# A gated mix of long convolution and local attention: the second half of the attention heads on blocks of 57 queries by 64 keys, in a new hand-written order

## The chip, the cores and the metric

The kernel runs on one core of a Trainium2 chip. Five engines work side by side and meet through semaphores: PE (TensorE, the matrix multiplier, whose weight loads are shown apart as PEld), DVE (VectorE), ACT (ScalarE), POOL (GpSimd) and SP (SyncE, which here only issues DMAs). PE writes only to PSUM, and ACT and DVE carry its results from there into SBUF. The metric is the device time of one execution in microseconds (us).

## The reference

Two branches share the input `x = A_q` (2048 rows, 640 columns) and are mixed row by row by a gate. Branch A multiplies a shifted key by a value, convolves the product over the whole sequence (an FFT in the reference) and multiplies by `q`. Branch B is attention with 32 heads of 20 columns, in which every query sees only 8 keys: its own row and the rows 2, 4, ... 14 above it.

```python
x = A_q
g = sigmoid((x * gate_w).sum(-1, keepdims=True))
# A: k_shift = 4-tap causal convolution of A_k; kv = k_shift * A_v
#    y = causal convolution of kv with ssm_k over 2048 rows (rfft, product, irfft, cut to S); y = y + kv * ssm_D
a = x * y
# B: q, k, v = x @ wqkv in 32 heads of 20
logits = einsum("bhsd,bhswd->bhsw", q, kg) * 20 ** -0.5     # kg: keys at s, s-2, ... s-14
o = einsum("bhsw,bhswd->bhsd", softmax(masked logits), vg)
b = o.reshape(B, S, D) @ wo
return g * a + (1 - g) * b
```

## The kernel before, in words

The even rows and the odd rows of `x` form two sequences of 1024, so that a query's keys are 8 neighbours. Attention cuts each sequence into 9 blocks of 114 queries (`BQ`), and a block needs 121 keys (`BK`): its own 114 and the 7 ahead of them. There are 18 blocks (`NB`) and 8 *sets* `t` of four heads. A set's keys and queries lie in `kb` and `qb`, the four heads at partitions 0, 32, 64 and 96, 20 rows of data and 11 rows of a mask each (`mm`): the mask makes the score of every pair outside the band so negative that its exponential is zero.

For a set, `score_gen` (L637) multiplies keys by queries into PSUM, 121 keys on the partitions by 114 queries on the columns, the four heads as four tiles of 32 rows of the array (L647); the 18 blocks go in five groups of 4, 4, 4, 3 and 3. ACT takes the exponential of each group in two instructions, two heads in each (L658), 912 or 684 columns of 121 partitions, into one of 9 slots (`NET`) of `ETall`. `pv_gen` (L664) uses each piece of `ETall` as the weights of a matmul whose moving operand is the head's 20 value columns and a column of ones (`VW`, L682; the extra columns of the next heads that it takes along are overwritten). DVE takes the reciprocal of the ones' column (L692) and multiplies (L694) into `oS`, which lies over `VW`. Matmuls at L652 write to columns that nobody reads.

The values `VW` are made by `vproj` (L526), one half of the heads each (`hp`), the keys and queries by `qkproj` (L573) into `stg`, from where DMAs on POOL's queue (on SP's for the first) place them into `kb` and `qb` (`fragger`, L623). When all sets are done, `op_tr` (L861) transposes `oS` through PE into `oT` and `outproj` (L877) multiplies by `wo` into `bl`.

Branch A runs in between: `conv` and `conv_v` on DVE (L472 to L491); `h_stream` and `u_stream` transform the filter and the product in two stages (L713 and L709 the first, L732 the second) in two passes `P`; the filter's results are copied once with the halves swapped by DMAs (`swaps`, L828: pairs of DMAs, a pair waits for the one before through a POOL copy, L822); `products` multiplies on DVE (L764); `inverse1` (L843) and `final` (L930) transform back. All evictions from PSUM that are a plain copy have the line of a helper, L244 on ACT and L246 on DVE. `gate` ends with four small DMAs on SP (L548) and three instructions on DVE (L551 to L553). `load_h` of pass 1 brings the filter's second half (`h_lin`, L324) into the place of the first.

The order is written by hand: every generator above is a stream, a letter in `ORDER` grants the stream's next step, and a minus ahead of it gives an eviction to DVE instead of ACT. The instructions of an engine stand in its queue in that order. PSUM is given out in four slots of two banks; a group of scores takes two slots, most other steps one or a half.

## Time and profile before

| | |
|---|---|
| time, median of 3 runs | 220.84 us (220.32 to 221.04) |
| the profiled execution | 219.82 us, of it 218.0 us from the first to the last instruction |
| PE busy | 205.2 us, 94% of the span, 3642 matmuls |
| PEld busy | 166.8 us, 76% |
| DVE busy | 183.4 us, 84%, 264 instructions |
| ACT busy | 173.5 us, 80%, 251 instructions |
| POOL busy | 50.8 us, 23% |
| mean granted clock of PE | 0.99 |

Matmuls are pipelined and a busy PE may wait between them, so that its share says little; what one matmul costs is read from the step between neighbours, or from a piece of the chain (a run of one line's matmuls, with its length in us). The mean of an instruction on ACT or DVE includes some 0.1 us in which the next has begun.

### The profile page before, as it was taken

How to read it: one execution, taken by the hardware profiler on the slowest of the kernel's cores; microseconds unless marked ns; L12 is line 12 of the kernel's file. 1: busy time of each engine (PE TensorE's matmuls, PEld its weight loads, DVE VectorE, ACT ScalarE, POOL GpSimd, SP SyncE). 2: the span in 40 equal slices, each digit the busy share in tenths (PEclk: the TensorE clock that was granted, in tenths of full speed). 3: DMA queues.
4: the chain of work that ended last, by engine and by line, in shares of the span. 5: the costliest groups of instructions: out<-in, count | busy, mean ns of one | idle time of the engine just before them, and what ended most of it. 6: DMA issues, size and time to landing. Idle time of an engine off the chain costs nothing.

```text
span 218.0 us, 8528 instructions
## 1 busy us (share of the span) xinstructions
PE 205.2 (94%) x3642; PEld 166.8 (76%) x3642; DVE 183.4 (84%) x264; ACT 173.5 (80%) x251; POOL 50.8 (23%) x129
## 2 busy tenths in 40 slices
PE   6999999999999999999997988999999999999990
PEld 3876987696677677656685766899888999998880
DVE  6647778997998998789897968998999997898782
ACT  0354387769998998989998988999899999487760
POOL 7980811460517045405420000000000000000000
PEclk9999999999999999999999699999999999999999
DMA  6999799699954993899984196767449064003544
GB/s 199 349 251 287 205 185 188 137 168 154 272 160 102 150 146 64 152 150 151 168 160 107 31 223 140 174 158 226 110 110 289 7 149 95 3 3 96 139 128 131
DMA packets 69049, 33.35 MB, mean 153 GB/s; under 512 B 51476, under 2 KB 66708, under 8 KB 69012
## 3 DMA queue, kind: packets, MB, share of 16 engines
q1 hardware_dynamic: 65684, 27.66, 62.0%
q0 software_dynamic: 2880, 4.90, 9.6%
q8 instruction: 28, 0.46, 1.0%
q10 hardware_dynamic: 448, 0.26, 0.4%
q14 instruction: 9, 0.07, 0.1%
HBM read 19.51 MB, written 2.62 MB: 102 GB/s over the span
## 4 chain that ended last, share of the span: by engine, by line
PE 66%; DVE 12%; ACT 6%; SPq 6%; DMA 5%; issue 3%; DVEq 0%; ACTq 0%
PE PS L573 16%; PE PS L526 12%; PE PS L877 10%; PE PS L843 8%; ACT ETall L658 5%; PE PS L682 5%; SPq L324 5%; PE PS L647 4%; PE PS L732 3%; DVE UC L246 3%; DMA h_lin<-in_A_ssm_k_dram 3%; DVE SX L246 3%; PE PS L930 2%; DMA WvT<-in_B_wqkv_dram 2%; PE PS L444 2%
## 5 line engine op out<-in xcount | busy, mean ns | idle before, releaser
L658 ACT ACTIVATE ETall<-PS 121x912 bf16<-121x912 f32 (+1 forms) x80 | 63.9, 865 | 6.4 <-PE PS L647 6.0
L573 PE MATMUL PS<-xT,Wqk 128*128 128x342 bf16 (+1 forms) x300 | 49.8, 310 | 0.7 <-ACT stg L244 0.3
L244 ACT CAST UC<-PS 128x1024 bf16<-128x1024 f32 (+2 forms) x49 | 44.4, 1030 | 4.0 <-DVE UC L246 3.1
L573 PEld LDWEIGHTS <-Wqk 128*128 128x128 bf16 x300 | 27.3, 97 | 14.6 <-issue 0.5
L526 PE MATMUL PS<-WvT,xT 128*121 128x320 bf16 x180 | 27.5, 301 | 0.6 <-DMA WvT<-in_B_wqkv_dram 0.3
L472 DVE TENSOR_TENSOR KX<-KX 128x1280 bf16<-128x1280 bf16 x32 | 25.3, 820 | 0.3
L526 PEld LDWEIGHTS <-xT 128*121 128x121 bf16 x180 | 23.5, 134 | 2.2 <-issue 0.4
L623 POOL DMA_DIRECT2D qb<-stg x29 | 14.5, 504 | 43.3 <-ACT stg L244 27.1
L877 PE MATMUL PS<-wo,oT 128*128 128x320 bf16 x160 | 24.5, 302 | 0.1
L244 ACT CAST stg<-PS 128x363 bf16<-128x363 f32 (+1 forms) x39 | 17.1, 472 | 8.5 <-PE PS L573 8.2
L877 PEld LDWEIGHTS <-oT 128*128 128x128 bf16 x160 | 21.0, 145 | 1.5 <-issue 0.5
L623 POOL DMA_DIRECT2D kb<-stg x36 | 18.0, 510 | 14.8 <-ACT stg L244 7.6
L732 PEld LDWEIGHTS <-G 64*128 64x128 bf16 x512 | 18.1, 93 | 3.8 <-issue 2.5
L682 PEld LDWEIGHTS <-ETall 121*128 121x128 bf16 x576 | 17.8, 97 | 1.6 <-issue 0.2
L682 PE MATMUL PS<-VW,ETall 121*128 121x63 bf16 (+2 forms) x576 | 18.5, 186 | 0.1
L843 PE MATMUL PS<-F,Hw 128*128 128x128 bf16 x160 | 18.1, 219 | 0.0
L843 PEld LDWEIGHTS <-Hw 128*128 128x128 bf16 x160 | 17.9, 114 | 0.0
L647 PE MATMUL PS<-qb,kb 31*128 31x114 bf16 x576 | 15.6, 212 | 2.3 <-ACT ETall L658 1.2
L246 DVE CAST UC<-PS 128x1024 bf16<-128x1024 f32 x13 | 15.3, 1220 | 2.6 <-ACT UC L244 1.2
L647 PEld LDWEIGHTS <-kb 31*128 31x128 bf16 x576 | 9.3, 93 | 10.3 <-issue 8.8
L246 DVE CAST SX<-PS 128x1024 bf16<-128x1024 f32 (+2 forms) x13 | 14.6, 1159 | 2.8 <-PE PS L732 1.7
L891 ACT ACTIVATE bl<-PS,omg 128x320 bf16<-128x320 f32 x30 | 15.4, 566 | 1.9 <-PE PS L877 1.4
(75 smaller groups left out, 329.9 us busy)
## 6 DMA issues: line engine op xcount, KB each, us to landing
xn<-in_A_q_dram SPq DMA_DIRECT2D x8, 320.0 KB
h_lin<-in_A_ssm_k_dram SPq DMA_DIRECT2D x16, 160.0 KB
vin<-in_A_v_dram SPq DMA_DIRECT2D x8, 320.0 KB
Hw<-H SPq DMA_DIRECT2D x8, 320.0 KB
q<-in_A_q_dram SPq DMA_DIRECT2D x8, 320.0 KB
Hw<-SX SPq DMA_DIRECT2D x8, 320.0 KB
kb<-stg POOLq DMA_DIRECT2D x28, 85.1 KB, 4.1
out_dram<-q SPq DMA_DIRECT2D x16, 120.0 KB
```

The source lines that it names most:

```text
L244: nc.scalar.copy(dst, src)
L246: nc.vector.tensor_copy(dst, src)
L472: eng.tensor_tensor(d, kin[:, n + 3 - j:n + 3 - j + m, :], w.to_broadcast([128, m, QC]), ALU.mult)
L526: nc.tensor.matmul(ps[0:BK, 0:320], lhsT=xT[:, dt, s0:s0 + BK], rhs=Wv[:, dt, 320 * hp:320 * hp + 320], start=(dt == 0), stop=(dt == NDT - 1))
L573: nc.tensor.matmul(ps[:, 0:n], lhsT=Wqk[:, dt, w, 128 * ft:128 * ft + 128], rhs=xT[:, dt, s0:s0 + n], start=(dt == 0), stop=(dt == NDT - 1))
L623: (nc.sync if near else nc.gpsimd).dma_start(dst[r0:r0 + rows, 0:wd], stg[fa - f0:fb - f0, 0:wd])
L647: nc.tensor.matmul(psum(g, h4 // 2)[:, h4 % 2, BQ * bb:BQ * bb + BQ], lhsT=kb[r:r + DH + NF, BK * b:BK * b + 128], rhs=qb[r:r + DH + NF, B ...
L658: nc.scalar.activation(ETall[0:BK, e, :, 0:BQ * nb], psum(g, k)[0:BK, :, 0:BQ * nb], ACT.Exp, scale=SCALE)
L682: nc.tensor.matmul(O[:, (b - b0) // 6, c0:c0 + 21 * nh], lhsT=ETall[0:BK, e, hh, BQ * bb:BQ * bb + 128], rhs=VW[0:BK, b, 4 * t + h4:4 * t ...
L732: nc.tensor.matmul(ps[:, c, 160 * jj:160 * jj + 160], lhsT=G[rows, j0 + jj, 64 - 64 * rr:192 - 64 * rr], rhs=Am[rows, rr].rearrange("p o ( ...
L843: nc.tensor.matmul(d, lhsT=st[(key, P)][:, c, o + il // 4, :, il % 4], rhs=M[:, k, :], start=(k == 0), stop=(k == 1), skip_group_check=True)
L877: nc.tensor.matmul(op, lhsT=oT[:, ft].rearrange("p h m a -> p a (h m)")[:, t, :], rhs=wo[:, ft, 320 * n:320 * n + 320], start=(ft == 0), s ...
```

## The change

For the sets 4 to 7 (`NEW = 4`) a block of 114 queries is halved: 57 queries (`SQ`) see 64 keys (`SK`), and the two halves lie one over the other on the 128 partitions of a score tile, at 0 and at 64. A set then has three groups of six blocks; a group's scores are 48 matmuls of 64 columns of weights by 57 (16 or 12 of 128 by 114 before), and its exponentials two instructions of 684 columns and 128 partitions: 6 for a set instead of 10. The product with the values becomes two matmuls on opposite quarters of the array, rows and columns 0 to 63 and 64 to 127. The values of the second half of the heads are made in the same stacked form, five pairs of matmuls of 64 columns instead of five of 121. In `ETall` 57 queries and 7 ones alternate for all sets, 8 slots instead of 9, and so the rows of `oS` lie at 0 to 56 and 64 to 120 in both halves. `op_tr` therefore multiplies by `pick`, the identity without the unused rows, in place of the transpose: its result is 32-bit, half as many columns fit a slot, and 5 evictions of 2048 columns become 10 of 1024. `ORDER` is the same up to the third set (`t = 2`) and new from there.

```diff
-NET = 9
-GROUPS = [[0, 1, 2, 3], [4, 5, 6, 7], [8, 9, 10, 11], [12, 13, 14], [15, 16, 17]]
+SQ = 57
+SK = 64
+NEW = 4
+NET = 8
+GROUPS = [[[0, 1, 2, 3], [4, 5, 6, 7], [8, 9, 10, 11], [12, 13, 14], [15, 16, 17]],
+          [[0, 1, 2, 3, 4, 5], [6, 7, 8, 9, 10, 11], [12, 13, 14, 15, 16, 17]]]
...
-222222244111p313333p31333333333333413333uu4uuu444444444444444u54vv55u-5555-55-55-55-5555555ssssuuvvvvvvvvvvttttttsssssssstttttts
+121111124oo4s14sp33ssss34p33v33433s4443s3s3344v3v33v34434-s434s3343v44-s4u5u55v-5u45v-55-5555v-5v55v555v55u5ttutvststssttttsssss
...
-    ETall = pR.tile([128, NET, 2, 3 * BQ + 128], BF, name="ETall")
+    ETall = pR.tile([128, NET, 2, 8 * SK], BF, name="ETall")
...
+        for i in range(2):
+            nc.gpsimd.tensor_copy(pick[:, SQ * i:SQ * i + SQ], ident[:, SK * i:SK * i + SQ])
...
+                    for i in range(2 if split else 0):
+                        nc.tensor.matmul(ps[SK * i:SK * i + SK, 0:320], lhsT=xT[:, dt, s0 + SQ * i:s0 + SQ * i + SK], rhs=rhs,
+                                         start=(dt == 0), stop=(dt == NDT - 1), tile_position=(0, SK * i), skip_group_check=True)
...
+                        for i in range(1 + split):
+                            c, q = BK * b + SQ * i, BQ * b + SQ * i
+                            nc.tensor.matmul(psum(g, h4 // 2)[SK * i:SK * i + SK, h4 % 2, bw * bb:bw * bb + bw] if split else psum(g, h4 // 2)[:, h4 % 2, bw * bb:bw * bb + bw],
+                                             lhsT=kb[r:r + DH + NF, c:c + (SK if split else 128)], rhs=qb[r:r + DH + NF, q:q + bw],
+                                             start=True, stop=True, tile_position=(r, SK * i), skip_group_check=True)
...
-                for n in range(0 if t < 6 else (2 if nb == 3 else (14 if t == 6 else 7))):
+                for n in range(0 if t < 6 else (((5 if t == 6 else 3)) if split else (2 if nb == 3 else (14 if t == 6 else 7)))):
...
+                                nh = min(2 if split else 3, 4 - h4)
...
+                                    nc.tensor.matmul(O[out, (b - b0) // 6, cs], lhsT=ETall[rows, e, hh, q0:q0 + (SK if split else 2 * SK)],
+                                                     rhs=VW[rows, b, 4 * t + h4:4 * t + h4 + nh, :].rearrange("p h e -> p (h e)"),
+                                                     start=True, stop=True, tile_position=(SK * i, SK * i), skip_group_check=True)
...
-            tr = psum(g, dt=BF)
-                nc.tensor.transpose(tr[:, par, BQ * j:BQ * j + w], oS[0:w, b, 128 * ft:128 * ft + 128], ident[0:w, 0:w])
-            r = yield Req("AD", dict(A=53.0 + 0.834 * 2048, D=70.0 + 0.52 * 2048), [g.done], give=g.banks)
+            for par in range(2):
+                tr = psum(g).rearrange("p a n -> p (a n)")
+                            nc.tensor.matmul(tr[:, q0:q1], lhsT=oS[0:BK, NBP * par + j, 128 * ft:128 * ft + 128],
+                                             rhs=pick[0:BK, q0 - BQ * j:q1 - BQ * j], start=True, stop=True, skip_group_check=True)
+                r = yield Req("AD", n=1024, deps=[g.done], give=g.banks)
```

The lines of the kernel move: L647 becomes L664, L658 becomes L676, L682 becomes L708, L526 is L537 for the first half of the heads and L539 for the second, L573 becomes L586, L732 becomes L758, L764 becomes L790, L861 becomes L889, L877 becomes L906, and the helper's L244 and L246 become L248 and L250.

ACT's queue from the exponentials of set 6 to the second stage of `u` (`SX` is the filter's second pass: 2x512 its first stage, 80x12 its second; `UC` 2x512 is the first stage of `u`), before:

```order
L658 ACTIVATE ETall<-PS 121x2x456 x6
L244 CAST SX<-PS 128x2x512 x4
L658 ACTIVATE ETall<-PS 121x2x342 x4
L658 ACTIVATE ETall<-PS 121x2x456 x6
L658 ACTIVATE ETall<-PS 121x2x342 x4
L244 CAST SX<-PS 128x80x12 x4
L244 CAST UC<-PS 128x2x512 x12
L244 CAST UC<-PS 128x80x12 x11
```

and now, from the last exponentials on:

```order
L676 ACTIVATE ETall<-PS 128x2x6x57 x8
L248 CAST SX<-PS 128x2x512 x4
L248 CAST UC<-PS 128x2x512 x3
L248 CAST SX<-PS 128x2x512
L248 CAST UC<-PS 128x2x512 x2
L248 CAST SX<-PS 128x80x12 x5
L248 CAST UC<-PS 128x2x512 x3
L248 CAST SX<-PS 128x80x12
L248 CAST SX<-PS 128x80x8
L248 CAST UC<-PS 128x2x512 x3
L248 CAST UC<-PS 128x80x12 x2
```

Four evictions of the filter's second pass stood amid the exponentials of set 6; now five of its first stage and all of its second stand behind the last exponentials, mixed with those of `u`.

DVE's queue from the end of the first stage of `u` over the evictions of `oT` into the products, before:

```order
L246 CAST UC<-PS 128x2x512 x8
L246 COPY oT<-PS 128x64x2x16 x3
L764 TENSOR_TENSOR H_289<-UC,H_289 128x80x12
L764 TENSOR_TENSOR Hw<-UC,Hw 128x80x12
L764 TENSOR_TENSOR H_289<-UC,H_289 128x80x12
L764 TENSOR_TENSOR Hw<-UC,Hw 128x80x12
L246 COPY oT<-PS 128x64x2x16 x2
```

and now:

```order
L937 TENSOR_SCALAR q_3378<-q_3378,g_nat 128x640 x2
L250 CAST UC<-PS 128x2x512
L250 CAST oT<-PS 128x32x2x16 x2
L790 TENSOR_TENSOR H_292<-UC,H_292 128x80x12
L790 TENSOR_TENSOR Hw<-UC,Hw 128x80x12
L790 TENSOR_TENSOR H_292<-UC,H_292 128x80x12
L250 CAST oT<-PS 128x32x2x16 x6
L790 TENSOR_TENSOR Hw<-UC,Hw 128x80x12
L250 CAST oT<-PS 128x32x2x16
L790 TENSOR_TENSOR H_292<-UC,H_292 128x80x12
L250 CAST UC<-PS 128x80x12
```

Nine of the ten halves of `oT` stand on DVE, with four products among them, where five whole ones and four products stood.

SP's queue around the gate, before:

```order
L324 DMA vin<-in_A_v_dram 32x64x80 x8
L548 DMA g_nat<-WvT 32x1x16 x4
L324 DMA h_lin<-in_A_ssm_k_dram 32x40x64 x8
L828 DMA Hw<-H_289 64x5x512 x2
L904 DMA q_2428<-in_A_q_dram 32x8x640
L828 DMA Hw<-H_289 64x5x512 x2
```

and now:

```order
L329 DMA vin<-in_A_v_dram 32x64x80 x8
L329 DMA h_lin<-in_A_ssm_k_dram 32x40x64 x8
L561 DMA g_nat<-WvT 32x1x16 x4
L854 DMA Hw<-H_292 64x5x512 x5
L933 DMA q_3378<-in_A_q_dram 32x8x640 x2
L854 DMA Hw<-H_292 64x5x512
```

The load of the filter's second half no longer stands behind the gate's DMAs; the loads of `q` moved behind the first DMA of the third pair of swaps.

More of the change, by code (lines that the diff above doesn't have):

```diff
@@ L259 @@
     ident = p0.tile([128, 128], BF, name="ident")
+    pick = p0.tile([128, BQ], BF, name="pick")
     F = p0.tile([128, 512], BF, name="F")
@@ L640, in score_gen @@
             kb, qb = ksets[t % 3], qsets[t % 3]
-            for gi, blocks in enumerate(GROUPS):
+            split = t >= NEW
+            bw = SQ if split else BQ
+            for gi, blocks in enumerate(GROUPS[split]):
                 nb = len(blocks)
-                g = yield Req("P", 0.0, [ev(f"set{t}")] + ([ev(f"near{t}")] if t < 2 else []), take=2, pe=(4 * nb, 11.8, 30.0, 11.8))
+                g = yield Req("P", 0.0, [ev(f"set{t}")] + ([ev(f"near{t}")] if t < 2 else []), take=2, pe=(4 * nb * (1 + split), 11.8, 30.0, 11.8))
                 for bb, b in enumerate(blocks):
@@ L654, in score_gen @@
+                w = 512 - bw * nb
+                for n in range(0 if t < 6 else (((5 if t == 6 else 3)) if split else (2 if nb == 3 else (14 if t == 6 else 7)))):
+                    nc.tensor.matmul(psum(g, 1)[:, 1, bw * nb:512], lhsT=mm[:, 0:128], rhs=mm[:, 0:w], start=True, stop=True, skip_group_check=True)
+                if gi == len(GROUPS[split]) - 1:
                     mark(f"sc{t}", g)
+                rows = 2 * SK if split else BK
                 for k in range(2):
                     e = s % NET
-                    r = yield Req("A", 68.0 + 0.834 * 2 * BQ * nb, [g.done, etfree[e], ev("ET")], give=[g.banks[k]])
@@ L658, in score_gen @@
-                    nc.scalar.activation(ETall[0:BK, e, :, 0:BQ * nb], psum(g, k)[0:BK, :, 0:BQ * nb], ACT.Exp, scale=SCALE)
+                    r = yield Req("A", 68.0 + 0.834 * 2 * bw * nb, [g.done, etfree[e], ev("ET")], give=[g.banks[k]])
+                    nc.scalar.activation(ETall[0:rows, e].rearrange("p h (c q) -> p h c q", q=SK)[:, :, 0:bw * nb // SQ, 0:SQ],
+                                         psum(g, k)[0:rows, :, 0:bw * nb].rearrange("p h (c q) -> p h c q", q=SQ), ACT.Exp, scale=SCALE)
@@ L666, in pv_gen @@
         for t in range(NT):
-            for gis, b0, na in PARTS:
-                mm_ = sum(4 * len(GROUPS[gi]) for gi in gis)
-                blocks = [b for gi in gis for b in GROUPS[gi]]
+            split = t >= NEW
+            groups = GROUPS[split]
+            for gis, b0, na in PARTS[split]:
+                mm_ = sum(4 * len(groups[gi]) for gi in gis) * (1 + split)
+                blocks = [b for gi in gis for b in groups[gi]]
                 g = yield Req("P", 0.0, [ev(f"e{t}{gi}{k}") for gi in gis for k in range(2)] + [ev(f"VW{t // 4}{b}") for b in blocks], take=1, half=na % 2,
@@ L677, in pv_gen @@
                         for hh in range(2):
-                            for bb, b in enumerate(GROUPS[gi]):
+                            for bb, b in enumerate(groups[gi]):
                                 h4 = 2 * hf + hh
                                 c0 = 84 * ((b - b0) % 6) + 21 * h4
-                                nh = min(3, 4 - h4)
-                                nc.tensor.matmul(O[:, (b - b0) // 6, c0:c0 + 21 * nh], lhsT=ETall[0:BK, e, hh, BQ * bb:BQ * bb + 128],
-                                                 rhs=VW[0:BK, b, 4 * t + h4:4 * t + h4 + nh, :].rearrange("p h e -> p (h e)"),
-                                                 start=True, stop=True, skip_group_check=True)
+                                nh = min(2 if split else 3, 4 - h4)
+                                cs = slice(c0, c0 + 21 * nh)
+                                for i in range(1 + split):
+                                    rows = slice(SK * i, SK * i + SK) if split else slice(0, BK)
+                                    out = slice(SK * i, SK * i + SK) if split else slice(0, 2 * SK)
+                                    q0 = SK * bb if split else 2 * SK * bb
+                                    nc.tensor.matmul(O[out, (b - b0) // 6, cs], lhsT=ETall[rows, e, hh, q0:q0 + (SK if split else 2 * SK)],
+                                                     rhs=VW[rows, b, 4 * t + h4:4 * t + h4 + nh, :].rearrange("p h e -> p (h e)"),
+                                                     start=True, stop=True, tile_position=(SK * i, SK * i), skip_group_check=True)
                         x = etfree[e]
```

57 lines of the change are left out of this document (28 added, 29 removed).

## The prediction

> **What bounds the kernel now.** I read the share of each engine by stretch first, then the chain of waits, then the groups of instructions, and last the queues around the places that move. The chain is nearly all PE's up to the gate (L539) and again from the first output projection on; the stretches:
>
> ```profile
> core 0: us, PE busy (x) PEld busy (x) DVE busy (x) ACT busy (x) POOL busy (x), PEclk, DMA share, GB/s
> 62.50:95.20 32.70, 32.52 (x547) 23.34 (x549) 28.69 (x44) 29.79 (x46) 12.24 (x38) 1.00 0.83 121
> 95.20:150.60 55.40, 50.62 (x1063) 41.38 (x1060) 48.59 (x56) 51.40 (x67) 7.72 (x18) 0.97 0.77 151
> 150.60:161.30 10.70, 10.59 (x235) 9.58 (x234) 10.35 (x13) 9.76 (x12) 0.37 (x2) 1.00 0.52 124
> 161.30:212.90 51.60, 51.35 (x1104) 47.18 (x1104) 46.71 (x79) 43.65 (x64) 0.00 (x0) 1.00 0.42 104
> ```
>
> Only in 95.2 to 150.6 is PE visibly idle, and there ACT is busy for 51.4 of 55.4 us. The exponentials are most of what ACT does there, and the change halves their columns. The pieces of the chain, in order of time, give the prices of PE's work (start, length, line, matmuls):
>
> ```profile
> 62.47 0.33 PE PS L713 x8
> 62.80 0.32 PE PS L647 x16
> 63.12 0.86 PE PS L573 x5
> 63.97 0.68 PE PS L526 x5
> ...
> 66.61 0.27 PE PS L647 x12
> ...
> 74.38 0.65 PE PS L682 x24
> 75.03 0.32 PE PS L647 x16
> 75.35 2.32 PE PS L573 x15
> ...
> 85.21 0.78 PE PS L713 x24
> ...
> 93.98 1.19 PE PS L539 x20
> ...
> 119.48 0.47 PE PS L652 x14
> ...
> 137.96 0.76 PE PS L682 x24
> ...
> 148.66 1.93 PE PS L709 x16
> 150.59 1.86 PE PS L861 x36
> 152.46 0.94 PE PS L732 x24
> ...
> 161.27 0.83 PE PS L877 x5
> ...
> 193.66 0.96 PE PS L930 x96
> ...
> 200.64 0.69 PE PS L930 x64
> ```
>
> Twelve scores take 0.27 us and sixteen 0.32, so one costs 0.0125 us and a piece 0.12 besides; L930 gives 0.0084 and 0.15 in the same way. I take 0.1 us for each change of tile shape, the price of which the trace thus shows twice. A product with the values costs 0.65 / 24 = 0.027 us, a matmul of qkproj about 0.148 (2.32 / 15, less the piece's 0.1).
>
> **The change, part by part.**
>
> ```profile
> L658 ACT ACTIVATE ETall<-PS 121x912 bf16<-121x912 f32 x48 | 41.9, 944 | 2.1 <-PE PS L647 1.9
> ...
> L526 PEld LDWEIGHTS <-xT 128*121 128x121 bf16 x180 | 23.5, 134 | 2.2 <-issue 0.4 <-DVE xT L246 0.4
> ...
> L658 ACT ACTIVATE ETall<-PS 121x684 bf16<-121x684 f32 x32 | 22.1, 745 | 4.3 <-PE PS L647 4.1
> ...
> L682 PEld LDWEIGHTS <-ETall 121*128 121x128 bf16 x576 | 17.8, 97 | 1.6 <-issue 0.2
> ...
> L539 PEld LDWEIGHTS <-wgz 128*32 128x32 bf16 x20 | 0.4, 96 | 0.6 <-issue 0.3
> ```
>
> *Exponentials.* 24 of 912 columns go (41.9 / 48 = 0.87 us each) and 8 more of 684 come (22.1 / 32 = 0.69): ACT loses 20.9 - 5.5 = 15.4 us. It is worth only what PE idles for.
>
> *Product with the values.* In sets 4 to 7, 288 matmuls become 576. A tile's turn now is 27 ns whether 21 or 63 columns move, so the loading of weights sets it. A load of 121 columns has 134 ns, one of 32 columns 96, one of 128 columns 97: the full 128 load in a faster way, and otherwise a column costs 38 / 89 = 0.43 ns. 64 columns then come to 96 + 14 = 110 ns, 13 over the load of now, and a tile's turn to 40 ns. Two tiles lie on different rows. Sixteen scores in 0.32 us, four tiles of rows at a time, show that loads on different rows overlap (one after another at 27 ns they would take 0.43), so I take 20 ns a matmul: 11.5 us against 288 x 0.027 = 7.8, **+3.7 us**. Bounds: 10 ns (0.96 / 96, L930, where 16 tiles turn) and 40 ns (no overlap), -2.0 and +15.2 us. I take 20 because the load is what L682 waits for.
>
> The Trainium skill, "TensorEngine Tiling (Array Packing)", section Restrictions and Gotchas, says that column tiling excludes Fast Weight Load, and so speaks against this part; the 32-column load of L539, no shorter than the full one, agrees. If 64 columns loaded as fast as 128 do, a pair would take 27 ns, the sum would fall by 576 x 6.5 ns = 3.7 us, and the time would be 219.2 in place of 222.9 us.
>
> *Scores.* 20 pieces (12 of 0.32, 8 of 0.27 us) become 12 of 48: 48 x 0.0084 + 0.1 = 0.5 us each by L930's price, 6.0 us for 6.0: **0**. Bounds: 0.48 us by L930's 96 in 0.96, and 0.96 by 0.020 as now: -0.2 to +5.5 us.
>
> *Values.* Five pairs replace five matmuls in 18 steps. L539 puts four of 512 columns side by side, 20 in 1.19 us, where 5 of 512 alone would take 0.136 x 512 / 320 x 5 = 1.09: pairing costs at most 9%, **+0.3 us** taken, +1.1 the upper end, 0 the lower.
>
> *Shapes.* In PE's order the tile shape changes 151 times instead of 130: 21 x 0.1 = **+2.1 us**.
>
> *Idle matmuls and transposes.* 71 matmuls at L652 (0.034 us each, 2.4) become 24 of 170 columns (170 / 320 x 0.136 = 0.072; 1.7): **-0.7 us**. 100 products with `pick` replace 90 transposes at the same width (1.86 / 36 = 0.05): +0.1, hidden where DVE is behind (below).
>
> So PE gains about 5.5 us of work. ACT and DVE keep their time for an instruction where only partitions grow (114 or 121 to 121 or 128). POOL gets two copies of 57 columns, far below the 2 us of its 2178-column copies, ahead of a queue that waits for `stg`; the shorter fill of `ETall` lies ahead of the first evictions. Eight slots for nine: every order here has the product of the first groups ahead of the exponential that reuses the slot, so I cost it at nothing; if that exponential came first, it would wait for 48 matmuls, 1.3 us.
>
> **The sum, in four stretches.** Both orders are the same to the first filter piece (62.47 above); seven of the changed value steps lie ahead of it, so it now stands at 63.0.
>
> *To the end of the last set, PE.* The order has there 125 matmuls of qkproj (18.5 us), 11 value steps (7.6), 112 old scores (1.4) and 576 new (4.8), 144 old products (3.9) and 576 new (11.5), 128 of L713 (3.6, 0.78 less 0.1 over 24), 128 of the filter's second stage (0.94 less 0.1 over 24: 4.5), the gate (1.1), the idle ones (1.7), and 83 changes of shape (8.3): 66.9 us. In 62.5 to 95.2, with ACT and DVE as loaded, the 547 matmuls come to some 31.7 of 32.7 us at these prices, so I add 1.5 for waits. Summed over their queues at the prices below, ACT has 45 us of work in these 68 and DVE some 53: neither binds. The last product ends at 131.4 (138.72 before); the last exponentials, with 4.3 us of PE's work behind their scores and 1.4 of their own, at 128.5.
>
> *Evictions, ACT and DVE.*
>
> ```profile
> 109.56 6.00 ACT L244 CAST H<-PS 128x960 bf16<-128x960 f32 x7
> ...
> 121.18 3.77 ACT L244 CAST SX<-PS 128x1024 bf16<-128x1024 f32 x4
> ...
> 120.39 4.78 DVE L246 CAST SX<-PS 128x1024 bf16<-128x1024 f32 x4 [0.21 <-PE PS L713]
> ...
> 157.86 2.35 DVE L246 COPY oT<-PS 128x2048 bf16<-128x2048 bf16 x2
> 160.12 0.66 DVE L764 TENSOR_TENSOR H<-UC,H 128x960 bf16<-128x960 bf16 x1
> 160.69 0.66 DVE L764 TENSOR_TENSOR Hw<-UC,Hw 128x960 bf16<-128x960 bf16 x1
> ```
>
> Behind the last exponential ACT has 16 evictions of 1024 columns (3.77 / 4 = 0.94), 6 of 960 (6.00 / 7 = 0.86) and one of 640 (0.6): 20.8 us. DVE has about as much. PE needs less here (80 of L709 at 0.11, which is 256 / 320 of L526's 0.136, and 128 of L732 at 0.035: 13.3), so `u`'s first stage is out of PSUM at 149.3. Before, PE itself ended it at 150.59: **of the 7 us won, the moved filter pass takes more than five back.**
>
> *`oT`, DVE.* Nine evictions at 1.13 us (157.86 to 160.12 is two; 32-bit words go at half the rate, half the columns) and four products at 0.57: 12.4 us, and 0.2 to start; five and four took 7.9. The output projection, which needs all of `oT`, starts at 161.9; before at 161.27.
>
> *The rest, PE.* From there the kernel took 218.0 - 161.27 = 56.7 us. 160 matmuls of the second stage stand behind that point now instead of 112, 48 x 0.035 = +1.7, less one piece: 58.3. DVE's 12.7 us of products behind `oT` end at 174.6, 55 output projections (7.5), those 160 (5.6) and the changes of shape, 13.8 us of PE's work ahead of `inverse1`, end at 175.7: no wait.
>
> 161.9 + 58.3 = 220.2 us of span, 2.1 over the 218.0. The profiled execution (219.82) is 1.0 under the median of the runs; on that median of 220.84 I forecast **222.9 us**.
>
> **The rivals.**
>
> *The product pair is cheap: faster.* If a matmul of the pair comes at L930's 10 ns, PE's first stretch is 5.8 us shorter, ACT and DVE still finish inside it, and everything behind moves up: 217.1 us. It decides at 2.1 us / 576 = 3.6 ns under my 20, that is below 16.4 ns. It ends faster by 1.7%. For it: 16 tiles do turn that fast. Against it: they load 32 columns, and four rows of tiles share the loading where here there are two.
>
> *The pair does not overlap: slower.* 40 ns a matmul: +11.5 us, 234.4 us. For it: nowhere in the kernel before do two tiles that differ in rows write the same PSUM bank, as these do. Against it: the overlap of L647.
>
> *PE goes on waiting.* In 95.2 to 150.6 ACT too was idle for 4.0 us (55.4 - 51.4), so the exponentials were not all that PE waited for. If those 4 us have another cause and stay, the time is 226.9 us. The swaps belong here:
>
> ```profile
> 116.10 1.38 SPq L828 DMA_DIRECT2D Hw<-H  x2
> ...
> 131.83 1.39 SPq L828 DMA_DIRECT2D Hw<-H  x2
> ...
> 137.38 2.17 SPq L828 DMA_DIRECT2D Hw<-H  x2
> ...
> 148.84 13.48 SPq L828 DMA_DIRECT2D Hw<-SX  x6
> ```
>
> A pair takes 5.5 us (131.83 to 137.38), and the eight follow one another. The first now stands behind the gate, which PE reaches at 113 instead of 94: pairs from 119, the third held by `q`'s loads until the filter's place is free (136.7), the fourth landed at 149, and four more at 171. The products of pass 1 need them at 174.6: 3 us to spare. The filter's load gains: it no longer waits for the gate.
>
> *Nothing that can be measured.* The time within 0.3% (0.7 us), about what a measurement of this kernel tells from no change: 2.1 us is a small rest of 5.5, 7 and 5.
>
> **How the numbers follow.** Forecast (a span 0.7 to 4 us longer) 0.42; cheap pair, with smaller waits counted in, 0.28; waits stay 0.13; no overlap 0.07; within 0.3% 0.10. The first, third and fourth are slower, with 0.05 of the first falling within 0.3%: slower 0.57, same 0.15, faster 0.28. The range goes from the cheap pair, 217.1, to the waits that stay, 226.9, with 2 us of the scores' upper end; it leaves out the missing overlap and the far end of a faster one. The forecast's own range is 221.5 to 225.
>
> **What would show it.** Right: L708 steps of about 20 ns, pieces of 96 near 2.0 us; L664 pieces of 48 near 0.5; the last L708 at about 132; evictions without a gap on ACT from 128 to 149; L906 first at 162 released by DVE `oT`. Wrong: L708 pieces of 96 near 1 us or 3.8; PE waits on ACT or the swaps in 95 to 130; a lower granted clock where sets 6 and 7 leave PE in small matmuls (0.97 over 95.2 to 150.6 before, 1.7 us of those 55.4).

## The result, and the profile after

The changed kernel takes 241.38 us (median of 4 runs, 239.99 to 246.64) against 220.94 for the kernel before: ratio 1.0901, 95% interval 1.082 to 1.0982. I had forecast slower, but 222.9 us: the direction came out and the size did not, by 18.5 us. Now and then an execution of one of these kernels is longer than the rest, and the ratios leave it out; the profiled one is the longest of its four (246.64 us, span 244.7, the others 238 to 240), so what is read below from behind the sets holds some 4 us that the others lack.

From the page: the busy row, PE's granted clock over 40 slices of 6.1 us, and the queue that brings instructions (transfers, MB, share of 16 DMA engines).

```profile
PE 220.3 (90%) x4271; PEld 174.2 (71%) x4271; DVE 185.5 (76%) x268; ACT 163.4 (67%) x236; POOL 51.6 (21%) x131
...
PEclk9999999999999999997955556999799999999798
...
q8 instruction: 33, 0.54, 1.0%
```

The same queue in the kernel before:

```profile
q8 instruction: 28, 0.46, 1.0%
```

ACT is busy for 163.4 us instead of 173.5, as meant. But PE's clock is at half from 123 to 151 us, and the stretches of the forecast, on the chip (columns as in the prediction), are these:

```profile
64.16:102.00 37.84, 37.84 (x716) 24.24 (x716) 33.72 (x49) 31.18 (x50) 15.02 (x44) 1.00 0.82 122
102.00:146.40 44.40, 37.02 (x1233) 29.83 (x1233) 23.82 (x30) 22.55 (x32) 4.56 (x11) 0.70 0.47 94
146.40:165.40 19.00, 18.55 (x243) 15.86 (x242) 16.71 (x17) 17.55 (x21) 0.19 (x1) 0.89 0.69 149
165.40:182.05 16.65, 11.38 (x198) 9.66 (x196) 13.91 (x15) 9.08 (x10) 0.37 (x2) 0.90 0.60 131
182.05:240.00 57.95, 54.29 (x1152) 49.37 (x1151) 49.60 (x83) 43.91 (x61) 0.56 (x1) 0.97 0.37 92
```

In the second row every engine has time to spare: DVE and ACT are busy for half of the 44.4 us, and PE, the bound, stands for 7.4 of them. Before, the end of the sets looked like this (one row of the same view), with ACT at 39.8 of 43.5:

```profile
95.20:138.72 43.52, 39.11 (x939) 30.71 (x936) 37.67 (x45) 39.78 (x54) 7.53 (x17) 0.96 0.78 140
```

What PE waits for, the chain says: "issue", time in which it waited for nothing that the profile shows.

```profile
103.88 1.63 PE PS L708 x96
...
106.66 1.92 issue
...
121.01 1.65 issue
...
145.03 1.39 PE PS L708 x48
...
160.39 10.55 DMA Hw<-H
171.06 0.66 DVE H L790
...
182.05 1.52 PE PS L906 x10
```

Six such pauses between 106 and 141 us (1.92, 0.60, 1.65, 1.02, 1.05 and 0.95) make 7.2 us. PE's timeline shows their beat; in brackets is the idle time ahead of a row:

```profile
131.46 0.28 PE L664 MATMUL PS<-qb,kb 31*64 31x57 bf16 x8 [1.02 <-issue]
131.66 0.60 PE L669 MATMUL PS<-mm 128*128 128x170 bf16 x3
132.20 2.73 PE L708 MATMUL PS<-VW,ETall 64*64 64x42 bf16 x96
134.86 0.37 PE L664 MATMUL PS<-qb,kb 31*64 31x57 bf16 x21
136.28 0.42 PE L664 MATMUL PS<-qb,kb 31*64 31x57 bf16 x27 [1.04 <-issue]
136.63 0.61 PE L669 MATMUL PS<-mm 128*128 128x170 bf16 x3
137.17 1.45 PE L708 MATMUL PS<-VW,ETall 64*64 64x42 bf16 x48
138.56 0.66 PE L664 MATMUL PS<-qb,kb 31*64 31x57 bf16 x48
139.14 0.47 PE L669 MATMUL PS<-mm 128*128 128x170 bf16 x2
140.56 0.30 PE L669 MATMUL PS<-mm 128*128 128x170 bf16 x1 [0.95 <-issue]
```

Between the first two pauses stand 8 + 3 + 96 + 21 = 128 matmuls, between the next two 27 + 3 + 48 + 48 + 2 = 128. Each has a weight load: 256 instructions. And the instruction queue made 33 transfers for 8542 matmuls and loads (28 for 7284 before), one for 259. So theory A: **PE's instructions arrive 256 at a time, and PE stops where it uses them up faster than the next come.** Its rivals: B, the swaps held behind the loads of `q`, the wait that I had priced at 226.9 us; and C, the half clock by itself.

### The profile page after: what moved, and what is told of

Same layout as the page of the kernel before. It is cut to its first block, busy times and chain, and to the rows that moved or that the text cites. A ratio compares the mean times of both kernels' runs of the same rounds, so it can differ in the third digit from the quotient of the medians.

```text
span 244.7 us, 9761 instructions
## 1 busy us (share of the span) xinstructions
PE 220.3 (90%) x4271; PEld 174.2 (71%) x4271; DVE 185.5 (76%) x268; ACT 163.4 (67%) x236; POOL 51.6 (21%) x131
## 4 chain that ended last, share of the span: by engine, by line
PE 74%; DMA 9%; DVE 5%; issue 5%; ACT 4%; SPq 1%; DVEq 0%; POOL 0%; POOLq 0%; ACTq 0%
PE PS L586 18%; PE PS L906 9%; PE PS L708 8%; DMA Hw<-H 7%; PE PS L869 7%; PE PS L539 6%; PE PS L537 6%; PE PS L758 5%; PE PS L664 5%; PE PS L739 3%; DVE oT L250 2%; PE PS L959 2%; DMA WvT<-in_B_wqkv_dram 2%; PE PS L735 2%; ACT ETall L676 2%
## 5 line engine op out<-in xcount | busy, mean ns | idle before, releaser
L676 ACT ACTIVATE ETall<-PS 121x912 bf16<-121x912 f32 (+2 forms) x64 | 50.3, 830 | 13.1 <-PE PS L664 10.2
L586 PE MATMUL PS<-xT,Wqk 128*128 128x342 bf16 (+1 forms) x300 | 50.6, 311 | 2.3 <-issue 1.9
L248 ACT CAST UC<-PS 128x1024 bf16<-128x1024 f32 (+2 forms) x47 | 43.9, 1003 | 12.5 <-PE PS L758 6.9
L586 PEld LDWEIGHTS <-Wqk 128*128 128x128 bf16 x300 | 26.7, 97 | 17.6 <-issue 4.1
L906 PE MATMUL PS<-wo,oT 128*128 128x320 bf16 x160 | 26.0, 314 | 1.1 <-DVE oT L250 1.1
L248 ACT CAST stg<-PS 128x363 bf16<-128x363 f32 (+1 forms) x38 | 17.1, 462 | 13.2 <-PE PS L586 13.0
L708 PEld LDWEIGHTS <-ETall 64*64 64x64 bf16 (+1 forms) x864 | 22.3, 122 | 4.6 <-issue 3.6
L758 PEld LDWEIGHTS <-G 64*128 64x128 bf16 x512 | 19.2, 97 | 8.7 <-issue 7.3
L708 PE MATMUL PS<-VW,ETall 64*64 64x42 bf16 (+4 forms) x864 | 23.6, 196 | 1.8 <-issue 1.6
L906 PEld LDWEIGHTS <-oT 128*128 128x128 bf16 x160 | 21.3, 147 | 3.1 <-issue 1.0
L250 DVE CAST UC<-PS 128x1024 bf16<-128x1024 f32 (+2 forms) x15 | 17.6, 1189 | 4.1 <-PE PS L735 1.8
L869 PE MATMUL PS<-F,Hw 128*128 128x128 bf16 x160 | 18.5, 219 | 0.0
L869 PEld LDWEIGHTS <-Hw 128*128 128x128 bf16 x160 | 17.9, 114 | 0.2
L664 PE MATMUL PS<-qb,kb 31*64 31x57 bf16 (+1 forms) x864 | 15.2, 214 | 2.1 <-issue 2.1
L664 PEld LDWEIGHTS <-kb 31*64 31x64 bf16 (+1 forms) x864 | 10.2, 110 | 9.5 <-issue 8.2
L718 DVE RECIPROCAL rd<-PS 121x48 f32<-121x48 f32 (+1 forms) x16 | 6.1, 382 | 13.4 <-PE PS L708 13.3
L920 ACT ACTIVATE bl<-PS,omg 128x320 bf16<-128x320 f32 x26 | 13.5, 542 | 3.9 <-PE PS L906 3.5
L248 ACT CAST H<-PS 128x1024 bf16<-128x1024 f32 (+2 forms) x13 | 12.3, 964 | 4.7 <-PE PS L758 4.7
```

Of the source, the lines that this page charges most:

```text
L248: nc.scalar.copy(dst, src)
L250: nc.vector.tensor_copy(dst, src)
L586: nc.tensor.matmul(ps[:, 0:n], lhsT=Wqk[:, dt, w, 128 * ft:128 * ft + 128], rhs=xT[:, dt, s0:s0 + n], start=(dt == 0), stop=(dt == NDT - 1))
L664: nc.tensor.matmul(psum(g, h4 // 2)[SK * i:SK * i + SK, h4 % 2, bw * bb:bw * bb + bw] if split else psum(g, h4 // 2)[:, h4 % 2, bw * bb:bw ...
L676: nc.scalar.activation(ETall[0:rows, e].rearrange("p h (c q) -> p h c q", q=SK)[:, :, 0:bw * nb // SQ, 0:SQ], psum(g, k)[0:rows, :, 0:bw * ...
L708: nc.tensor.matmul(O[out, (b - b0) // 6, cs], lhsT=ETall[rows, e, hh, q0:q0 + (SK if split else 2 * SK)], rhs=VW[rows, b, 4 * t + h4:4 * t ...
```

## The experiments

Times are medians beside the kernel before on the same chip, 220.6 to 222.2 us; in brackets stand the ratio and its interval. In the expectations, A1 is theory A, A2 its contrary; C1 says that the clock goes by how much of the array moves, C2 by idle time.

**The supply by itself (m1, and m2 with loads beside it).** A kernel of PE's small matmuls alone:

```diff
+    for pairs, rows, cols, moving, at in PARTS:
+        for n in range(40):
+            nc.tensor.matmul(PS[:, 4, :], lhsT=a[:, 0:128], rhs=a[:, 128:640], ...)
+        for n in range(pairs):
+            r, c = at[n % len(at)]
+            nc.tensor.matmul(PS[c:c + cols, r // 32, 0:moving], lhsT=a[r:r + rows, 0:cols], rhs=a[r:r + rows, 128:128 + moving], tile_position=(r, c), ...)
```

> A kernel of its own that leaves out the whole computation: PE alone, six streams of one form of matmul each with its own weights (32 rows by 32 columns, 20 moving, on 16 tiles, 1280 times; 64 by 64, 42 moving, on the two tiles of the product, 1024; 31 by 64, 57 moving, on the eight tiles of the scores, 1024; 121 by 128, 21 moving, 768; the same with 63 moving, 768; 128 by 128, 160 moving, 512), each behind 40 matmuls of 128 by 128 by 512, with no load under way. Theory A1 (PE's instructions come in blocks of 256, that is 128 matmuls with their loads, and a block takes 4.3 to 4.8 us from the use of the last): the first three streams, 8.4 to 17 ns a matmul in the kernel, run at 34 to 37 ns a matmul with a pause every 128; the fourth and fifth (27 ns, 3.5 us a block) pause for about 1 us a block; the last (67 ns) does not pause. Theory A2 (PE pauses for another reason, as semaphores or PSUM): no pauses here at all, 1280 matmuls of the first stream in 10.8 us. Theory C1 (the clock goes by how much of the array's columns and rows move in a window of 3.4 us): the fourth stream falls to half clock although PE never idles for long, the fifth stays at full. Theory C2 (it goes by idle time): the fourth and the fifth have the same clock.

The first stream on the timeline, with no semaphore and no load anywhere near (the rows of weight loads between them are left out):

```profile
12.67 1.63 PE L53 MATMUL PS<-a 32*32 32x20 bf16 x183
16.79 1.20 PE L53 MATMUL PS<-a 32*32 32x20 bf16 x128 [2.48 <-issue]
...
20.52 1.20 PE L53 MATMUL PS<-a 32*32 32x20 bf16 x128 [2.53 <-issue]
...
23.97 1.20 PE L53 MATMUL PS<-a 32*32 32x20 bf16 x128 [2.25 <-issue]
```

128 matmuls run in 1.2 us, and then PE stands for 2.3 to 2.8. Behind the first 183, 1097 matmuls take the 30.3 us from 16.79 to 47.08, 3.5 us for 128. The first five streams by stretch:

```profile
12.67:47.08 34.41, 11.96 (x1281) 11.10 (x1282) 0.00 (x0) 0.00 (x0) 0.00 (x0) 0.55 0.02 4
57.38:85.05 27.67, 25.02 (x1025) 24.41 (x1026) 0.00 (x0) 0.00 (x0) 0.00 (x0) 0.62 0.02 4
95.15:120.87 25.72, 10.38 (x1025) 9.49 (x1026) 0.00 (x0) 0.00 (x0) 0.00 (x0) 0.62 0.02 4
131.72:152.70 20.98, 20.69 (x769) 20.49 (x769) 0.00 (x0) 0.00 (x0) 0.00 (x0) 0.59 0.02 5
162.95:185.51 22.56, 22.56 (x769) 22.50 (x769) 0.00 (x0) 0.00 (x0) 0.00 (x0) 1.00 0.02 4
```

The second and third, 1024 matmuls, take 27.7 and 25.7 us, 3.5 and 3.2 for 128 with what lay ready at the start: the step hardly depends on what the matmul costs. A2 is out. The price is lower than the 4.3 to 4.8 us that I expected, so that the fourth and fifth streams (27 and 29 ns a matmul, 3.5 and 3.8 us a block) fit in and do not pause. They also decide between C1 and C2: neither idles, the one with 21 moving columns ran at half clock (0.59 with its beginning), the one with 63 at full.

> The same streams on PE with 64 loads of 1.3 MB each on SP's queue beside them. Theory A1: if the blocks of instructions share the DMA engines with the data, a block takes longer than in the run without loads (over 5 us), and the first three streams slow down in proportion; if the blocks' time is not shared, both runs have the same steps. Theory A2: no pauses in either.

The only difference is 64 loads of 1.3 MB on SP's queue:

```diff
-TRAFFIC = 0
+TRAFFIC = 64
```

The first stream's timeline and the first three stretches again:

```profile
13.11 1.63 PE L53 MATMUL PS<-a 32*32 32x20 bf16 x183
20.06 1.20 PE L53 MATMUL PS<-a 32*32 32x20 bf16 x128 [5.32 <-issue]
27.08 1.20 PE L53 MATMUL PS<-a 32*32 32x20 bf16 x128 [5.82 <-issue]
```

```profile
13.11:70.37 57.26, 11.95 (x1281) 11.11 (x1282) 0.00 (x0) 0.00 (x0) 0.00 (x0) 0.53 1.01 422
81.40:125.20 43.80, 27.25 (x1025) 26.41 (x1026) 0.00 (x0) 0.00 (x0) 0.00 (x0) 0.55 1.01 421
136.13:182.16 46.03, 10.47 (x1025) 9.56 (x1026) 0.00 (x0) 0.00 (x0) 0.00 (x0) 0.54 1.01 422
```

With the DMA engines full (share 1.01) a block takes 5.5 to 5.9 us (50.3 us for 1097 in the first stream): the data slow the instructions. The kernel's sets (share 0.47) lie between: 2466 instructions in 44.4 us are 4.6 us a block. The kernel before used 1875 in 43.5, 5.9 a block.

The Trainium skill, "Runtime: NRT & Kernel Launch", section Instruction fetch mechanics, says that instructions are refilled in blocks of 256, and here the traces agree; it also calls the cost of such a boundary mostly hidden, and there they do not: 2.3 to 2.8 us of each block stay in sight in the first stream of m1, and 4.7 to 5.8 us beside full DMA engines.

**Fewer instructions in the kernel.** One matmul instead of two for a block and head, in the product (e4), in the scores (e7), and in both (e8):

```diff
-                                for i in range(1 + split):
-                                    nc.tensor.matmul(O[out, ...], lhsT=ETall[rows, e, hh, q0:q0 + (SK if split else 2 * SK)], ...)
+                                q0 = min(SK * bb, 4 * SK) if split else 2 * SK * bb
+                                nc.tensor.matmul(O[:, ...], lhsT=ETall[rows, e, hh, q0:q0 + 2 * SK], ...)
```

> The changed kernel, but in sets 4 to 7 the product with the values is one matmul of 128 rows by 128 columns per block and head instead of two of 64 by 64: it leaves out the separation of the two halves, so 288 matmuls and 288 weight loads are gone and each left takes about 27 ns where a pair took 34. PE's work by its own prices is 2 us less. Theory A: with 576 instructions fewer in 102 to 146 us, some two of the nine blocks of 256, the pauses get fewer, the clock is full for longer because a full tile does twice the work per instruction, and the time falls by 6 to 12 us, to 229 to 235 us. Theory B: only the 2 us of PE's work show, 238 to 241 us.

230.79 us, 10.6 less (1.0465, 1.0393 to 1.0537). The sets' stretch:

```profile
102.00:134.20 32.20, 27.32 (x940) 22.69 (x940) 22.81 (x30) 21.25 (x31) 3.84 (x10) 0.91 0.66 121
```

The last product ends at 134.2 instead of 146.4, for 2 us less of PE's work by its prices. Still 4.4 us a block. The clock is back too (0.91 for 0.70), so this run alone does not tell the supply from the clock; the pace of the blocks does, below.

```diff
-                        for i in range(1 + split):
-                            nc.tensor.matmul(psum(g, h4 // 2)[SK * i:SK * i + SK, ...], lhsT=kb[..., c:c + SK], ...)
+                        nc.tensor.matmul(psum(g, h4 // 2)[:, ...], lhsT=kb[..., c:c + 128], ...)
```

> The changed kernel, but in sets 4 to 7 one matmul of 128 columns of weights by 57 makes the scores of a block and head instead of two of 64 (the second half's scores are left out, and the exponentials of these sets are those of zero): 288 matmuls and their loads are gone, as many as in the run with one product, but the cheapest ones, 0.0105 us each. Theory A1 (instructions, in blocks of 256 that cost 4.3 to 4.5 us each where PE uses them faster): 576 / 256 x 4.4 = 9.9 us less, 229 to 234 us, the same as leaving out the products. Theory A2 (PE's work): 288 x 0.0105 = 3 us less, 237 to 240 us.

232.83 us, 8.6 less (1.0521, 1.0461 to 1.0581): nearly the same gain from the same number of instructions, though these matmuls are the cheapest ones.

> Both reductions at once: one matmul for the scores and one for the product with the values of a block and head in sets 4 to 7 (the separation of the halves is left out; 1152 instructions fewer, 106 more than the kernel before has). Theory A1: both steps add up until the supply of instructions no longer binds; the last product ends at 128 to 133 us, near the 131.4 that I forecast, pauses of over 1 us and half clock are gone from the sets, and the time is 221 to 227 us, what is left over the forecast being in the evictions of oT and the end of the kernel. Rival (the order or the exponentials' layout costs the sets their time): the last product stays at 138 us or later and the time at 229 or more.

224.56 us (1.0163, 1.0104 to 1.0222), 16.8 less. The sets:

```profile
101.40:129.50 28.10, 24.63 (x722) 19.85 (x721) 22.72 (x30) 20.60 (x30) 4.24 (x10) 0.94 0.71 135
```

The last product stands at 129.5; the order, the layout and the short exponentials are all still there. So of the 20.4 us that the change costs, 16.8 go with the 1152 instructions of the halves. By the prices of the forecast their work alone was 5 us (288 x 0.0105 + 2).

**More instructions before (e6).** The kernel before with 480 narrow matmuls that nobody reads:

```diff
+                for n in range(24 if t >= 4 else 0):
+                    h4, r = n % 4, 32 * (n % 4)
+                    nc.tensor.matmul(psum(g, h4 // 2)[:, h4 % 2, BQ * nb:BQ * nb + 16], lhsT=kb[r:r + DH + NF, 0:128], rhs=qb[r:r + DH + NF, 0:16], ...)
```

> The kernel before with 480 additional matmuls, 24 behind each group's scores of sets 4 to 7, of the scores' form with 16 moving columns, into columns that nobody reads: 960 instructions and 480 x 0.0125 = 6 us of PE's work in a stretch where PE idled for about 5 of 55 us. Theory A1: pauses of 0.5 to 2 us appear behind the groups where 256 instructions are used in under 4.3 us, the clock falls to half in some windows, and the time is 228 to 238 us. Theory A2 (only PE's work counts): 221 to 226 us, without pauses beyond those that are there (0.69 us the longest).

227.3 us (226.50 to 229.20, without one of 662), ratio 1.0257 (1.0172 to 1.0341). That lies between the two ranges, and the 5 us over the kernel before are no more than the 6 us of work. Pauses did appear in the chain:

```profile
134.08 1.81 issue
...
140.47 0.80 issue
```

It does not decide alone: the kernel before uses a block in 5.9 us and had room. At the 4.6 us a block of this run's sets (2826 instructions from 95.2 to 145.8 us), its 43.5 us would have held 546 of the 960 more.

**The clock.** Wide idle matmuls, which keep the array busy with few instructions:

```diff
+                for n in range(4 if split else 0):
+                    nc.tensor.matmul(psum(g, 1)[:, 1, :], lhsT=mm[:, 0:128], rhs=F[:], ...)
-                for n in range(0 if t < 6 else (((5 if t == 6 else 3)) if split else ...)):
-                    nc.tensor.matmul(psum(g, 1)[:, 1, bw * nb:512], lhsT=mm[:, 0:128], rhs=mm[:, 0:w], ...)
```

The first version (e5) moved `xT` instead of `F`:

> The changed kernel with 48 idle matmuls of 128 by 128 by 512 columns in sets 4 to 7, four ahead of each group's scores, in place of 24 of 170 columns behind those of sets 6 and 7: 10.2 us of PE's work at full clock for 1.7. Theory C1 (clock by the share of the array in use): the long stretch at half clock (27 us in the profiled execution) is gone, the work in it takes some 10 us less and the idle ones some 8 more, so that the time is 237 to 243 us with a mean clock over 0.97. Theory A1 alone (the blocks of instructions bound the stretch and the clock matters little): the idle matmuls fill pauses, hardly any pause over 0.5 us is left in 106 to 146 us, and the time stays within 2 us of 241. Theory C2 (idle time): the clock still falls after every pause of over 1 us.

244.51 us (240.55 to 245.87), but this says nothing of the clock: the swaps' target `Hw` lies where `xT` was, and SP waited 13.8 us for the last idle matmul to let go of it. With `F` (e11):

> The changed kernel with 48 idle matmuls of 512 columns in sets 4 to 7 once more (four ahead of each group's scores, in place of 24 narrow ones), now with F as what they move, which lies in memory to the end; the first time they read xT and so held back the swaps, whose target takes its place. If the half clock is what costs the sets their time, the last product ends by 138 us or earlier and the time falls to 232 to 237 us; if the supply of instructions costs it and the clock only goes along, the clock is full over most of 102 to 146 us, the last product still ends at 144 to 148 us and the time is 238 to 243 us.

241.87 us, ratio 1.0838 (1.0764 to 1.0912), which the changed kernel's 1.0901 (1.082 to 1.0982) cannot be told from. The clock and the sets:

```profile
PEclk9999999999999999999999959999999999999999
```

```profile
103.40:145.90 42.50, 39.04 (x1263) 26.73 (x1263) 25.38 (x32) 23.09 (x35) 6.00 (x14) 0.92 0.50 99
```

The clock is back (0.92 for 0.70) and 8.5 us of idle work more are done, and the last product still ends at 145.9: 4.3 us for 256 instructions. This end does not decide by itself, because the idle work may have taken what the full clock gave; the expectation of e5 has C1 at 237 to 243 us for that reason. The pace of the blocks decides. Where a pause ends, a new block has come; two such rows of the changed kernel, ahead of the spell at half clock:

```profile
118.47 0.36 PE L758 MATMUL PS<-H,G 64*128 64x160 bf16 x5 [0.60 <-issue]
...
122.66 0.58 PE L708 MATMUL PS<-VW,ETall 64*64 64x42 bf16 x27 [1.65 <-issue]
```

That block took 4.19 us, nearly all of it at full clock. The next four, at half clock from 123 us on, end with the pause ahead of 140.56 (in the timeline above): 17.9 us, 4.48 each (509 matmuls on record). One block of e11 at full clock:

```profile
131.89 0.32 PE L666 MATMUL PS<-qb,kb 31*64 31x57 bf16 x30 [0.50 <-issue]
...
135.89 1.03 PE L660 MATMUL PS<-F,mm 128*128 128x512 bf16 x2 [1.52 <-issue]
```

It took 4.00 us, and in e9 (below), at half clock, the blocks from 132.00 to 136.00 and on to 139.73 us took 4.00 and 3.73. So a block comes hardly sooner at full clock. I estimate that the half clock cost 0.3 to 0.5 us for each of those four blocks, 1 to 2 us in all, and at most 1 us more behind them, of the 15 us by which the sets end later than forecast. It went along with the pauses and had a small part in the time.

**The order.** (e3) The loads of `q` behind the fourth pair of swaps:

```diff
-L854 DMA Hw<-H_292 64x5x512 x5
-L933 DMA q_3378<-in_A_q_dram 32x8x640 x2
-L854 DMA Hw<-H_292 64x5x512
-L933 DMA q_3378<-in_A_q_dram 32x8x640 x2
+L854 DMA Hw<-H_292 64x5x512 x6
...
+L933 DMA q_3378<-in_A_q_dram 32x8x640 x4
```

> The changed kernel with the four loads of q behind the fourth pair of swaps on SP's queue instead of behind the first half of the third; nothing else moves. Theory B (the order): the four pairs land by about 150 us, the products and the evictions of oT no longer wait for Hw, the first output projection (182 in the profiled execution) starts at 171 to 174 and the time falls by 8 to 11 us, to 230 to 233 us. Theory A: PE still ends sets 4 to 7 at about 146 and the second stage of u behind them; what the swaps give back is under 5 us, 236 to 241 us.

240.17 us, 1.0814 (1.0736 to 1.0892): at most a little. What it took away had looked large among SP's waits in the changed kernel:

```profile
SPq L933 <- PE PS L739: 15.1, 1, 15.1
```

But PE ended `u`'s first stage only at 165.4 (165.3 without the hold), and of the whole wait DVE saw these 2.06 us:

```profile
171.06 0.66 DVE L790 TENSOR_TENSOR H<-UC,H 128x960 bf16<-128x960 bf16 x1 [2.06 <-DMA Hw<-H]
```

Without the hold, DVE has hardly a gap in that stretch (busy for 13.79 us), and it takes 14.0 us instead of 16.65:

```profile
165.30:179.30 14.00, 9.98 (x196) 8.42 (x195) 13.79 (x15) 8.99 (x10) 0.68 (x2) 1.00 0.50 119
```

B is a small part.

(e1) The new blocks in the old order (of `ORDER`, each set's letters for two groups taken out, those of `oT` doubled):

> The changed kernel with the order of the kernel before: of each set from the fifth on the second and fourth group's letters are taken out, and each half of an eviction of oT stands behind the other. Theory A (PE runs out of instructions, and the small matmuls of the split blocks then keep the granted clock low): the 629 additional matmuls are still there, so PE still pauses for 1 to 2 us at places where the profile shows no wait, the clock still falls to half in sets 5 to 7, and the time is 230 to 238 us. Theory B (the new order costs, by the swaps held behind the loads of q): the blocks alone cost what was forecast for PE, +5.5 us of work mostly beside ACT, and the time is 219 to 225 us, without the 15 us wait of SP ahead of the loads of q.

236.36 us (1.0724, 1.0665 to 1.0784), as A expected: 15.7 us of the cost come without the new order.

(e2) The old blocks in the new order:

```diff
-NEW = 4
+NEW = 8
```

> The changed kernel with NEW = 8, so that all sets have blocks of 114 queries, in the new order; the letters of the two groups that a set then has more stand behind the second and the third group. ACT has its 15.4 us of exponentials back. Theory A (instructions and clock): PE's additional matmuls are gone, so no pauses of over 1 us and no long stretch at half clock; what is left is the order's part and ACT's, 222 to 230 us. Theory B (the order): the swaps still wait behind the loads of q for about 15 us, and with ACT's longer work the time is 234 to 245 us.

240.27 us (1.0917, 1.0844 to 1.0991). A's number failed and B's came, but not by B's way: the sets ended only at 145.0, ahead of any wait for the swaps, PE and ACT waiting for each other in turn with ACT's longer exponentials in an order not made for them. It separates nothing.

(e14) The new blocks in the old order, with one score and one product:

> The new blocks in the order of the kernel before, with one matmul for the scores and one for the product of a block and head (the halves are not kept apart), so with 106 instructions fewer than the kernel before and 15 us fewer exponentials on ACT. If the additional instructions were all that the blocks cost in the old order (15.7 us there), it is 218 to 223 us, and below 220.1 the shorter exponentials would be worth something by themselves; if the blocks cost something else (the values in pairs, the longer way of oT through 32-bit evictions), it is 223 to 229 us.

227.16 us (1.0245, 1.0182 to 1.0309): 9.2 less than with the halves, and still 5.7 over the kernel before. The stretch from the end of `u`'s first stage to the first output projection says why:

```profile
152.70:168.50 15.80, 11.76 (x245) 9.95 (x242) 15.80 (x17) 10.43 (x13) 0.60 (x2) 1.00 0.62 159
```

15.8 us, all of it DVE's, where the kernel before took 10.67 (150.60 to 161.27): 5.1 us for `oT` in ten evictions of 32-bit columns.

(e9) The end of the order as before, each group of the last transform followed by output projections:

```diff
-ttutvststssttttssssssttttttttttttsssststststststsststsstttstststssts
+uvttttttssssssssttttttssssssttttttsssssttttttssssttttttssssttttttsss
```

> The changed kernel with the end of the order arranged as in the kernel before: from the first step of the last transform on, each of its six groups of 64 or 96 small matmuls is followed by a batch of output projections, where the changed order lets groups follow one another. Theory A1: the pauses of 1.15 and 2.2 to 2.5 us in the last transform go, and with them the window at half clock: 3 to 5 us less, 236.5 to 238.5 us, 57 to 58 us from the first output projection to the end. Rival: the end is longer for another reason and nothing changes, 240 to 242.5 us.

241.89 us (1.0938, 1.0878 to 1.0998): the rival's number. The 2.5 us pause of the last transform is gone, but the kernel ended 6.1 us behind its last matmul (234.7 of 240.8) instead of 4.7.

**The kernel before, improved?** Two ways to spare it instructions. Wide idle matmuls on `xT` (e10):

```diff
+                for n in range(1 if t >= 5 else 0):
+                    nc.tensor.matmul(psum(g, 1)[:, 1, :], lhsT=mm[:, 0:128], rhs=xT[:, 0, X0:X0 + 512], ...)
-                for n in range(0 if t < 6 else (2 if nb == 3 else (14 if t == 6 else 7))):
-                    nc.tensor.matmul(psum(g, 1)[:, 1, BQ * nb:512], lhsT=mm[:, 0:128], rhs=mm[:, 0:w], ...)
```

> The kernel before with 15 idle matmuls of 512 columns, one ahead of each group's scores of sets 5 to 7, in place of 71 narrow ones behind those of sets 6 and 7: 112 instructions fewer, 3.2 us of PE's work in place of 2.4. If instructions and the window at half clock cost the kernel before something too (pauses of 0.36 to 0.69 us and 3.4 us at half clock in its profile), the time falls by 0.5 to 2 us, to 219 to 220.3 us; if ACT alone sets the end of that stretch, it stays within 0.7 us of 220.8.

235.99 us (1.0678, 1.0629 to 1.0727), outside both. SP's waits name the reason, the held `xT` again (L649 is the score behind the last idle matmul, which starts at 137.04 us; the first swap is issued at 137.45):

```profile
SPq L827 <- PE PS L649: 20.4, 1, 20.4
```

With `F` (e12), and with no idle matmuls at all (e13):

> The kernel before with 15 idle matmuls of 512 columns that move F, in place of its 71 narrow ones: 112 instructions fewer. If the first version of this was slow only because xT was held, the 15 us of it are gone; and if pauses and the window at half clock cost the kernel before something too, the time is 219 to 220.3 us, else 220.3 to 221.5.

> The kernel before without its 71 idle matmuls: 142 instructions and 2.4 us of PE's work fewer in sets 6 and 7. If the clock needs them, windows at half clock appear between 120 and 140 us and the time is 221.5 to 224 us; if instructions weigh more, it is 219.5 to 220.5.

223.12 us (1.0084, 1.0049 to 1.012) and 221.6 us (1.0015, 0.9978 to 1.0052). `F` takes the 13 us back, but neither is faster, and e12 lies above both of its ranges: taking 112 or 142 instructions out of the kernel before gains nothing. Without idle matmuls the sets have one spell of 3.4 us at half clock, as they have with them. No version found here beats it.

## Why the prediction was wrong, step by step

The direction came out, but for the smaller part: what the forecast counted against the change (the moved filter pass, the longer way of `oT`) is left in e8, which takes 3.8 us more than the kernel before, 1.7 of them above the forecast's 2.1. The other 16.6 us of the 20.4 go with the instructions of the halves, of which the forecast held 5 us of work and not the supply. For that part the direction came out by luck.

- **The step that failed: "To the end of the last set, PE".** I added up PE's work (66.9 us) and put 1.5 us on it for waits; the stretch took 82.2 us (64.16 to 146.40). The prices in it were right or better than taken, the values' apart; the 1.5 came from a stretch with 547 matmuls in 32.7 us, 7.7 us for 256 instructions, where PE never came near its supply. The step counted the additional matmuls by their time and not as instructions: 2466 in 44.4 us, at 4.3 to 4.6 us for 256. e4, e7 and e8 show it by taking instructions away, and the pace of the blocks, 4.0 to 4.2 us at full clock and 3.7 to 4.8 at half, shows that the clock had little part in it.
- *Product, 20 ns taken:* 1.63 us for 96 at full clock, 17 ns. The two tiles do overlap, so neither the missing overlap (40) nor the cheap pair (10) came true as a price. The 27 ns for a pair that I set against them did not come either: it is 34. A load of 64 columns took the 110 ns that I had worked out (median of L539), one of 128 columns 97 (L586). The rule of the Trainium skill that I weighed, in "TensorEngine Tiling (Array Packing)", section Restrictions and Gotchas, agrees with that.
- *Scores, 0:* 48 in 0.50 us, as worked out from L930. That price was also the trap: 96 instructions in half a microsecond.
- *Values, +0.3 us:* L539 takes 3.58 us for 48, so that a step of ten comes to 0.73 us without the change of shape, against 0.68: +0.8 us over the 18 steps, inside the bounds.
- *Exponentials, -15.4 us on ACT:* 64.0 us became 50.3 (L658's 41.9 + 22.1 before, all of L676 after), -13.7. ACT's idle time grew accordingly, 13.1 us of it ahead of L676, 10.2 for the scores.
- *Lower granted clock:* named among the signs and priced at 1.7 us before; it was 27 us long and, by the pace of the blocks, worth some 1 to 3 us in the sets.
- *Evictions behind the last product, 17.9 us (131.4 to 149.3):* from 146.4 to the last eviction of `u`'s first stage at 166.7, 20.3 us, part of it at half clock; 19.0 in e11. Somewhat short.
- *`oT`, 12.6 us:* 15.4 from there to the first output projection, with the 2.06 us for `Hw` in it; without the hold of the swaps 12.9 (166.5 to 179.3), as worked out.
- *The rest, 58.3 us:* 57.95 to the last matmul and 4.7 behind it. 60.1 in e11 (178.10 to 238.2). Of the 2 to 4 us over, pauses for instructions in the last transform (2.50 us the longest) look like one part, but e9, in which that one is gone, was no faster; the cause stays open.
- *Start, 63.0 for the first filter piece:* 64.16; it lay at 62.5 to 65.7 over the kernels here, changed or not.
- *"PE goes on waiting", 226.9 us:* its sentence was right, that the third pair is held by the loads of `q`, and so was nearly the time of a pair (6.16 us in the chain, 5.5 taken). As a price it was too low for the kernel and too high for itself: e3 gained 1.2 us by the medians and 1.9 by the ratios, inside the uncertainty.

Open is what the new order costs by itself: 5 us separate the two orders with the new blocks (241.4 and 236.4), some 4 of it behind the first output projection, and no run takes that stretch apart. With one score and one product the sign turns: the new order (e8, 224.6, ratio 1.0163) is ahead of the old one (e14, 227.2, 1.0245). So the new order is not worse in itself; with the instructions of the halves it is, and by which step stays open.

## What to carry to other kernels

Count PE's instructions as well as their time. In this kernel, with the DMA engines about half busy, a stretch with more than 256 in some 4.5 us, that is matmuls under about 35 ns each with their loads, went at the pace of the blocks, and there splitting tiles cost in full even though the tiles ran side by side; with quiet DMA engines the price of a block was 3.2 to 3.5 us, with full ones 5.5 to 5.9. In a trace it shows as "issue" on PE every 128 matmuls, and at first sight as a fallen clock. And before an idle or auxiliary instruction reads a tile, see whose place that tile holds.
